# The softmax sums' steps of a fused FNet and window-attention kernel placed farther apart, and the first projection rows prepared behind the attention instead of inside it

## Chip, cores and metric

One core of a Trainium2 chip. The metric is the device time of one launch in microseconds. All times below are of the kernel before the change, and all line numbers in this part are those of its profile.

## What is computed

The sequence has S = 2048 rows of D = 512, in f32. A gate mixes a Fourier mixing layer with sliding-window attention:

```python
a = x @ dft_hid_re.T;  b = x @ dft_hid_im.T
y = dft_seq_re @ a - dft_seq_im @ b                    # spectral branch
q, k, v = split(x @ wqkv)                              # 32 heads of 16
scores = q @ k.T / 4,  kept where 0 <= i - j < 256
o = softmax(scores) @ v @ wo                           # attention branch
g = sigmoid((x * gate_w).sum(-1))
out = g * y + (1 - g) * o
```

The DFT matrices are inputs, loaded as cr and ci. All products run as three matmuls on split operands: each f32 operand is cast to a high part (a CAST on ACT) and a low part (a subtraction on DVE), and high by high, high by low and low by high are added up in PSUM.

## The kernel before

**The loop.** Attention goes over 128 blocks k (8 groups of 4 heads by 16 row blocks of 128 keys), each in two half blocks p = 0, 1. The loop counts n; the row maxima of block n are worked out 11 blocks ahead of block k = n - 11. A half block holds: scores for the row maxima (PE L426, DVE L430, "s_pair"), a piece of the dense stream ("fill"), the transposed scores (PE L486), their exp (ACT L489) and the window's mask (POOL L492 and L496), and pieces of the dense stream again. Every few blocks a "visit" multiplies by v (PE L513). The dense stream holds the projections, the spectral branch and, towards the end, the long DFT products `dc` (PE L270 and L282), whose operands are loaded as `raw` from cr and ci and split at L653. What is done per four blocks is called a u (0 to 31).

**The row maxima's way.** The maxima of four blocks (`rows`) go through DRAM: `m_scr<-rows`, then two loads `ring0<-m_scr`, which put them into the operand of the t matmuls at L486.

**The row sums' way.** After the last visit of u = k//4 - 1, eight steps stand in the list `later`, each at a number of half blocks counted from 2n: o_take (ACT copies the block o out of PSUM, L528, into a buffer `os` or `ev`), o_store (SP stores four rows of sums to `l_scr`, 8 KB), o_sums (SP loads them as 128x16), o_turn (DVE reciprocal, L541), o_back (SP stores them), o_load (SP loads them broadcast into an `ev`), o_out (POOL multiplies, L555) and o_end (four SP stores to `o_scr`). The buffers: `os` is one of the two v tiles' space vst0 and vst1 for u from 2 to 23, else one of the five `ev` buffers, which the spectral branch's pieces (`r_scr`) use as well.

**What sets the order.** While attention runs, every engine works in the order in which the code is written (a manual schedule). SP issues nearly all transfers (helper at L60) in that one order, so a transfer that has to wait for its buffer or its data holds all behind it. At the end of attention, `attention_done` closes the manual schedule for all engines but PE; what is written behind that point is placed by a scheduler on the other engines.

**The end.** The output projection (L1008 its products, seven instead of eight per pair of row blocks, by sums and differences) works on pairs of row blocks. A pair needs its rows of o (`oraw<-o_scr`), their sums (POOL L959 to L962; of the first pair DVE does them), their split (ACT and DVE, L84 and L89) and `rt`, loaded from r_scr, into which DVE adds the result (L1012). `tail_step` counts steps t of the dense stream behind attention, and BEGIN lists the step at which each pair's products begin. LAST is the number of the pair (15, 14), whose row block 15 is finished by the kernel's last 12 matmuls (L631). Tokens (L289, L308, L312, L613) are tiny ACT copies that mark when a `dc` bank is free again; PE waits for them.

**The first pair's preparation.** In the kernel before, the load of the first pair's rows (first_load), their sums (first_sums, on DVE) and splits (split_a(0), first_split) are called inside the attention loop, at blocks 124 to 128, by the dictionary BEFORE_END.

Of the kernel before, what the change touches and what calls it, by code (L numbers as in the profile page):

```python
# [7 lines left out]
F32 = mybir.dt.float32  # L8
# [6 lines left out]
P = 128  # L15
# [3 lines left out]
NG = 4  # L19
# [5 lines left out]
HV = 17  # L25
# [3 lines left out]
WARM = 10  # L29
BEHIND = 5  # L30
SWITCH = 7
LAST = 5
FILL_FIRST, FILL_PAIR, FILL_T = 12, 16.3, 12


# [1 line left out]
def fnet_window_mix(ctx: ExitStack, tc: tile.TileContext, xT, x, wqk, wv, wr, wi, cr, ci, wo, gw, out):  # L37
    nc = tc.nc

    const = ctx.enter_context(tc.tile_pool(name="const", bufs=1))  # L40
# [18 lines left out]
    def ld(dst, src):  # L59
        mark("sp", nc.sync.dma_start(dst, src))  # L60
# [8 lines left out]
    def mark(e, ins):  # L69
        last[e] = ins.ins  # L70

    @contextmanager
    def behind(*engines):
        with ExitStack() as es:
            for e in engines:
                if free and e in last:
                    es.enter_context(tc.issue_after(last[e]))
            yield
# [3 lines left out]
    def split(hi, lo, raw, act=False):  # L82
        if act:
            nc.scalar.copy(hi, raw)  # L84
        else:
            cast = (nc.gpsimd if act is None else nc.vector).tensor_copy(hi, raw)
            if act is None:
                mark("pool", cast)
        return nc.vector.tensor_sub(lo, raw, f(hi))  # L89
# [104 lines left out]
    vst = [const.tile([P, 8 * NG, HV], F32, name=f"vst{b}") for b in range(2)]  # L194
# [108 lines left out]
    def all_rows():  # L303
        H = Halves
        if H.part not in H.ended:
            while H.upper and H.upper[0][0] < H.part:
                pop()
            nc.scalar.copy(token, H.ps[:1, :1])  # L308
        while H.upper:
            pop()  # L310
        if H.part not in H.ended:
            nc.scalar.copy(token, H.ps[:1, :1])  # L312
        while H.due:
            H.due.pop(0)[1]()
        H.whole = True
# [205 lines left out]
    sums_t = [const.tile([P, 16], F32, name=f"sums{i}") for i in range(2)]  # L521

    def o_take(u):
        if 2 <= u < 24:
            o = const.tile([P, 8 * NG * HV], F32, name="os", tag=f"vst{u % 2}")[:, :512]
        else:
            o = ev.tile([P, 512], F32, name="ev")
        mark("act", nc.scalar.copy(o, OT.pop()))  # L528
        OS[u] = [o]
# [317 lines left out]
    def tail_step():  # L847
        t = next(clock)
        for i, begin in enumerate(BEGIN):
            if t == begin + 2:  # L850
# [7 lines left out]
            if i > 3 and t == max(0, begin - 9):  # L858
                wo_load(i)

    BEGIN = range(2, 26, 3)

    def flat(i):
        return ring[i].rearrange("r p s -> r (p s)")
# [6 lines left out]
    def os_spot(m, b, n=1):  # L871
        if m == 6 and b:
            at_c = 3 * S + 528
        else:
            at_c = (4 + m % 3 + 3 * (m == 6)) // 2 * S + 16 + 512 * ((m % 3 + (m == 6)) % 2) + 1024 * b
        t = flat(0 if m < 3 or m == 6 and b else 1)[:, at_c:at_c + 512 * n]
        return t if n == 1 else t.rearrange("p (m s) -> p m s", m=n)

    def halves(t):
        if len(t.shape) == 2:  # L880
            return t[:, :256], t[:, 256:]
        if len(t.shape) == 3:
            return t[:, :, :256], t[:, :, 256:]
        return t[:, :, :, :256], t[:, :, :, 256:]
# [7 lines left out]
    def wo_fetch(c):  # L892
        RAW[c] = [const.tile([P, 8 * NG * HV], F32, name="tw", tag=f"vst{j}")[:, :512] for j in range(2)]
        for j in range(2):
            ld(RAW[c][j], wo[j][:, HALVES[c]])
# [3 lines left out]
    def spare():  # L899
        return quarters(spared, 4)  # L900
# [8 lines left out]
    def fin_split(c, m):  # L909
        split(fin(m, 0, c), fin(m, 1, c), DIFF[c][m], True)  # L910

    def attention_done():
        all_rows()
        in_order.close()
        free.append(True)
        last.clear()
        ctx.enter_context(tc.manual_schedule(engines={mybir.EngineType.PE}))
        while later:
            later.pop(0)[1]()
        RT.append(const.tile([P, 6, 512], F32, name="rt", tag="home"))  # L920
        new = const.tile([P, NB * 4 * HV + 16], F32, name="oraw", tag="vall"), \
            at.tile([P, 4, WIN], F32, name="pt", bufs=4).rearrange("p a b -> p (a b)")
        ORAW[:0] = [t[:, 512 * c:512 * c + 512] for t in new for c in range(2)]
        r_load(0)
        wo_load(1)
        r_load(1)
        for i in range(2, 4):
            wo_load(i)
        FIN.append(True)
# [7 lines left out]
    def wo_load(i):  # L937
        pair = [15, 14] if i == LAST else [wait.pop(0) for _ in range(2)]
        raw = []
        for tb in pair:  # L940
            raw.append(ORAW.pop(0))
            ORAW.append(raw[-1])
            ld(raw[-1].rearrange("p (g t) -> p g t", g=NG),
               o_scr[tb // 4][:, :, tb % 4 * P:tb % 4 * P + P].rearrange("g p t -> p g t"))
        O[i] = pair, raw

    def first_load():
        ORAW.extend(const.tile([P, 8 * NG * HV], F32, name="oraw", tag=f"vst{b}")[:, :512] for b in range(2))
        wo_load(0)

    def r_load(i):
        k = 4 if i == LAST else i % 2 * 2
        R[i] = RT[0][:, k], RT[0][:, k + 1]
        for tb, t in zip(O[i][0], R[i]):
            with behind("sp"):
                ld(t, r_scr[2 if i == LAST else 1][tb])

    def sums(eng, s1, s2, s3, s4, a, b):
        eng.tensor_add(s1, b[:, :256], b[:, 256:])  # L959
        eng.tensor_sub(s3, a[:, :256], b[:, :256])  # L960
        eng.tensor_sub(s2, s1, a[:, :256])
        eng.tensor_sub(s4, a[:, 256:], s2)  # L962
# [9 lines left out]
    def first_sums():  # L972
        EX[0] = spare()
        sums(nc.vector, *EX[0], *O[0][1])

    def split_a(i):
        a, b = O[i][1]
        split(*halves(os_spot(0, i % 2, 2)), a.rearrange("p (m t) -> p m t", m=2), True)
        split(*halves(os_spot(2, i % 2)), b[:, 256:], True)

    def first_split(m):
        split(*halves(os_spot(m, 0)), EX[0][m - 3], True)
# [14 lines left out]
    def wo_begin(i):  # L997
# [27 lines left out]
        def rest():  # L1025
# [8 lines left out]
            for tb, r in zip(pair, (r1, r2)):  # L1034
                if i == LAST:
                    mixed[tb] = r
# [46 lines left out]
    summed = 0  # L1083
    later = []

    BEFORE_END = {(124, 1): first_load, (126, 1): first_sums, (127, 0): lambda: split_a(0)}
    for c, k in enumerate((111, 117)):
        BEFORE_END[k, c] = lambda c=c: wo_fetch(c)
        BEFORE_END[k + 2, 1 - c] = lambda c=c: wo_diffs(c)
        for j, m in enumerate((0, 1, 2, 4, 6, 5, 3)):  # L1090
            at_j = 2 * (k + 3) - c + j
            BEFORE_END[at_j // 2, at_j % 2, 0] = lambda c=c, m=m: fin_split(c, m)
    for j, m in enumerate((3, 5, 4, 6)):
        BEFORE_END[((127, 0, 0), (127, 1), (127, 1, 0), (128, 0))[j]] = lambda m=m: first_split(m)

    def ahead_of_end(*key):
        if key in BEFORE_END:
            with behind("t", "sp"):
                BEFORE_END[key]()

    for n in range(NU + LAG + 1):
        k = n - LAG
        ring_ahead(n + 1)
        if n % 4 == 1 and 9 <= n < 25:
            c = n // 4 - 2
            need(("v", 4 * c + 3))
            v_load(c)
        due = k > summed and (k % 4 == 0 or k == NU or k % 2 == 0 and not more)
        for p in range(2):
            if n < NU:  # L1110
                s_pair(n, p)
            fill(n)
            if p and due:
                visit(summed, k)
                summed = k
                if k % 4 == 0:
                    u = k // 4 - 1
                    G, sb = divmod(u, 4)
                    if G < 2 * NG - 1:
                        for c in [sb - 1] * (sb > 0) + [3] * (sb == 3):  # L1120
                            v_load(4 * (G + 1) + c)
                    later += [(2 * n + at, lambda do=do, u=u: do(u)) for at, do in
                              ((2, o_take), (3, o_store), (5, o_sums), (7, o_turn), (8, o_back), (10, o_load),
                               (13, o_out), (15, o_end))]
                    later.sort(key=lambda x: x[0])
                if k < NU:
                    t_pair(k, 0)
            if 0 <= k < NU and (p or not due):
                t_pair(k, p)
            ahead_of_end(k, p)  # L1130
            ahead_of_end(k, p, 0)
            fill(n)
            for at_n, at_p, do in TURN:
                u, j = divmod(n - at_n, 4)
                if p == at_p and j == 0 and 0 <= u < 32:
                    do(u)
            while later and later[0][0] <= 2 * n + p:
                later.pop(0)[1]()
# [47 lines left out]
```

## Time and profile before

| | us |
|---|---|
| median of 3 runs | 898.5 (895.81 to 898.92) |
| the profiled execution | 901.72 |
| its span | 900.0 |
| PE busy | 856.3 |
| DVE, ACT, POOL busy | 544.3, 405.1, 278.3 |
| moved by DMA | 167.62 MB, mean 186 GB/s |

The mean granted clock of PE was 0.979. The span begins with the first instruction and ends with the last transfer. The waits are lists of "engine line waited for: us in total, times, longest us"; SPq is SyncE's queue, whose instructions issue transfers. In the timelines a row is start, length, engine, line, operation, tiles (out<-in), and in brackets the idle time before it with what ended it. From about 74 us to 788 us the program is in the attention loop; from there on it is in the tail.

### The profile page before, as it was taken

Reading aid. Unit: us, or ns where it says so; the run is one execution under the profiler, and the core shown is the slowest. Engines: PE = TensorE matmul, PEld = TensorE weight load, DVE = VectorE, ACT = ScalarE, POOL = GpSimd, SP = SyncE. Lnnn points to the kernel's source line nnn. Section 1 sums busy time; section 2 is a strip of 40 time slices with the busy share of each in tenths; the row PEclk is TensorE's granted clock in tenths of the full one; section 3 lists DMA queues with packets and bytes.
Section 4 is the critical chain, followed back from the end, with each engine's and each line's share of the span. In section 5 each row is a group of like instructions: output and inputs, shape, how many; then the busy total and the mean of one; then the engine's idle time right before and its main releaser. Section 6 shows DMA issues by size and latency. Waiting matters only on the chain.

```text
span 900.0 us, 21479 instructions
## 1 busy us (share of the span) xinstructions
PE 856.3 (95%) x7641; PEld 734.0 (82%) x7641; DVE 544.3 (60%) x1607; ACT 405.1 (45%) x1017; POOL 278.3 (31%) x561
## 2 busy tenths in 40 slices
PE   8999999999989999999999999989899999949998
PEld 7988887777866888889999889868698887738987
DVE  5485666665656566656656666635567675536873
ACT  4423554445533454555455544433254456522320
POOL 7001223233322233333233332322234335423420
PEclk9999999999999999999999999989999999979999
DMA  7988688768778328765666569888786744566721
GB/s 231 254 233 203 168 202 246 236 169 221 208 184 251 87 80 217 176 146 140 165 163 166 160 193 278 211 206 285 194 199 173 208 131 121 154 174 214 235 94 71
DMA packets 110123, 167.62 MB, mean 186 GB/s; under 512 B 38720, under 2 KB 48448, under 8 KB 110016
## 3 DMA queue, kind: packets, MB, share of 16 engines
q1 hardware_dynamic: 109584, 165.60, 67.0%
q8 instruction: 60, 0.98, 0.5%
q10 hardware_dynamic: 432, 0.66, 0.3%
q14 instruction: 47, 0.39, 0.1%
HBM read 113.51 MB, written 52.69 MB: 185 GB/s over the span
## 4 chain that ended last, share of the span: by engine, by line
PE 72%; DMA 15%; DVE 5%; ACT 3%; issue 2%; SPq 2%; POOL 0%; DVEq 0%; ACTq 0%; POOLq 0%
PE dc L270 28%; PE dab L270 8%; PE o L513 7%; PE dqk L270 7%; PE s L426 5%; PE dv L270 4%; PE t L1008 4%; PE t L486 4%; PE dc L282 4%; DMA l_scr<-os 3%; DMA qk_scr<-home 2%; DMA ring<-qk_scr 2%; SPq L60 2%; DVE junk L430 2%; DMA raw<-ci 1%
## 5 line engine op out<-in xcount | busy, mean ns | idle before, releaser
L430 DVE CUSTOM_DVE_ANT_0 junk<-s,mask 128x384 bf16<-128x384 f32 (+2 forms) x512 | 270.4, 528 | 164.0 <-PE s L426 104.5
L270 PE MATMUL dc<-big,hi 64*128 64x512 f32 x1802 | 362.7, 396 | 3.4 <-ACT hi L653 3.4
L270 PEld LDWEIGHTS dc<-big,hi 64*128 64x128 f32 x1802 | 240.8, 188 | 10.9 <-ACT hi L653 3.8
L270 PE MATMUL dc<-big,lo 64*128 64x512 f32 x900 | 248.0, 396 | 0.3 <-DVE lo L653 0.2
L489 ACT ACTIVATE pt<-t 128x384 f32<-128x384 f32 (+2 forms) x400 | 164.1, 475 | 132.6 <-PE t L486 118.4
L492 POOL TENSOR_SCALAR_AFFINE_SELECT pt<-pt 128x256 f32<-128x256 f32 x200 | 86.8, 434 | 396.7 <-ACT pt L489 370.3
L270 PEld LDWEIGHTS dc<-big,lo 64*128 64x128 f32 x900 | 134.8, 188 | 3.8 <-DVE lo L653 1.1
L426 PE MATMUL s<-ring,ring 48*128 48x384 f32 (+2 forms) x512 | 127.8, 349 | 4.3 <-ACT pt L489 2.0
L653 DVE TENSOR_TENSOR lo<-raw,hi 128x512 fp32r<-128x512 f32 x142 | 106.7, 755 | 23.9 <-ACT hi L653 17.4
L653 ACT CAST hi<-raw 128x512 fp32r<-128x512 f32 x142 | 87.9, 626 | 73.1 <-PE dc L270 28.4
L270 PE MATMUL dab<-hi,big 64*128 64x512 f32 x512 | 116.5, 409 | 3.9 <-DVE home L98 3.4
L270 PE MATMUL dqk<-big,hi 64*128 64x512 f32 x480 | 112.8, 395 | 1.5 <-DVE home L96 1.0
L486 PE MATMUL t<-ring,ring 50*128 50x384 f32 (+2 forms) x512 | 108.9, 347 | 5.4 <-DVE ml L430 5.3
L426 PEld LDWEIGHTS s<-ring,ring 48*128 48x128 f32 x512 | 85.1, 187 | 18.5 <-DVE ml L430 6.1
L270 PE MATMUL dab<-lo,big 64*128 64x512 f32 x256 | 94.9, 405 | 0.0
L486 PEld LDWEIGHTS t<-ring,ring 50*128 50x128 f32 x512 | 68.3, 186 | 24.9 <-DVE ml L430 11.3
L270 PE MATMUL dqk<-big,lo 64*128 64x512 f32 x240 | 88.6, 398 | 0.0
L270 PEld LDWEIGHTS dab<-hi,big 64*128 64x128 f32 x512 | 78.4, 192 | 9.4 <-DVE home L98 4.9
L270 PEld LDWEIGHTS dqk<-big,hi 64*128 64x128 f32 x480 | 73.0, 185 | 8.2 <-DVE home L98 2.3
L496 POOL TENSOR_SCALAR_AFFINE_SELECT pt<-pt 128x256 f32<-128x256 f32 x176 | 74.5, 423 | 0.0
L513 PE MATMUL o<-pt,vall 128*32 128x384 f32 (+2 forms) x1104 | 72.6, 393 | 0.9 <-POOL pt L492 0.9
L489 ACT ACTIVATE home<-t 128x384 f32<-128x384 f32 (+2 forms) x112 | 45.4, 469 | 51.8 <-PE t L486 48.7
(120 smaller groups left out, 1069.0 us busy)
## 6 DMA issues: line engine op xcount, KB each, us to landing
qk_scr<-home SPq DMA_DIRECT2D x64, 256.0 KB
ring<-qk_scr SPq DMA_DIRECT2D x128, 128.0 KB
raw<-cr SPq DMA_DIRECT2D x32, 512.0 KB
raw<-ci SPq DMA_DIRECT2D x32, 512.0 KB
r_scr<-ev SPq DMA_DIRECT2D x44, 256.0 KB
ab_scr<-home SPq DMA_DIRECT2D x20, 512.0 KB
big<-ab_scr SPq DMA_DIRECT2D x20, 512.0 KB
ring<-qk_scr SPq DMA_DIRECT2D x128, 64.0 KB
```

The source lines that it names most:

```text
L60: mark("sp", nc.sync.dma_start(dst, src))
L270: nc.tensor.matmul(ps, lhsT[r], rhs[r], start=start, stop=stop, tile_position=(64 * i, 0), skip_group_check=True)
L282: return nc.tensor.matmul(ps, lhsT, rhs, start=start, stop=stop, skip_group_check=True)
L426: nc.tensor.matmul(pss[h][:, :w], ring[0][r, pair, j * BQ:(j + 1) * BQ], ring[1][r, pair, k0:k0 + w], start=True, stop=True, tile_position ...
L430: mark("dve", nc.vector.tensor_tensor_reduce(out=junk[:, :w], in0=pss[h][:, :w], in1=mask[:, WIN - w:], scale=1.0, scalar=3e38, op0=OP.add ...
L486: nc.tensor.matmul(pss[h][:, :w], ring[1][r, pair, q0:q0 + BQ], ring[0][r, pair, q0:q0 + w], start=True, stop=True, tile_position=(64 * h, 0))
L489: mark("t", nc.scalar.activation(pt[:, 2 * p + h, :w], pss[h][:, :w], AF.Exp, scale=-1.0))
L492: nc.gpsimd.affine_select(a, a, pattern=[[0, 2], [1, 128]], compare_op=OP.is_ge, fill=0.0, base=0, channel_multiplier=-1)
L496: nc.gpsimd.affine_select(a, a, pattern=[[0, 2], [-1, 128]], compare_op=OP.is_gt, fill=0.0, base=0, channel_multiplier=1)
L513: nc.tensor.matmul(OT[0][32 * t:32 * t + 32, q - sb * 512:e - sb * 512], vall[:, 4 * HV * kb + HV * t:4 * HV * kb + HV * t + 32], PT[n][:, ...
L653: return fn(*args)
L1008: nc.tensor.matmul(ps, o[:, a, c], fin(n, b, c), start=start and c == 0 and a + b == 0, stop=c == 1 and a == 1, skip_group_check=True)
```

## The change

1. The steps' places in half blocks behind 2n go from 2, 3, 5, 7, 8, 10, 13, 15 to 2, 3, 6, 9, 10, 13, 17, 19 (o_take, o_store, o_sums, o_turn, o_back, o_load, o_out, o_end).
2. The copies rotate over three buffers: vst0, vst1 and an `ev`, by u % 3, up to u = 24 (from 25 on all are `ev`).
3. first_load, first_sums, split_a(0) and the first_splits are no longer called inside the loop but in attention_done, behind the close of the manual schedule, and the list `later` is emptied behind the loads of rt and of the next pair's rows, not ahead of them.
4. BEGIN goes from steps 2, 5, 8, ... 23 to 6, 9, 12, ... 27, and LAST from 5 to 4.

```diff
-LAST = 5
+LAST = 4
...
     def o_take(u):
-        if 2 <= u < 24:
-            o = const.tile([P, 8 * NG * HV], F32, name="os", tag=f"vst{u % 2}")[:, :512]
+        if 2 <= u < 25 and u % 3 < 2:
+            o = const.tile([P, 8 * NG * HV], F32, name="os", tag=f"vst{u % 3}")[:, :512]
...
-    BEGIN = range(2, 26, 3)
+    BEGIN = range(6, 30, 3)
...
         ctx.enter_context(tc.manual_schedule(engines={mybir.EngineType.PE}))
-        while later:
-            later.pop(0)[1]()
         RT.append(const.tile([P, 6, 512], F32, name="rt", tag="home"))
...
+        first_load()
         ORAW[:0] = [t[:, 512 * c:512 * c + 512] for t in new for c in range(2)]
         r_load(0)
         wo_load(1)
         r_load(1)
+        while later:
+            later.pop(0)[1]()
+        first_sums()
+        split_a(0)
+        for m in (3, 5, 4, 6):
+            first_split(m)
...
-    BEFORE_END = {(124, 1): first_load, (126, 1): first_sums, (127, 0): lambda: split_a(0)}
+    BEFORE_END = {}
...
-    for j, m in enumerate((3, 5, 4, 6)):
-        BEFORE_END[((127, 0, 0), (127, 1), (127, 1, 0), (128, 0))[j]] = lambda m=m: first_split(m)
...
                     later += [(2 * n + at, lambda do=do, u=u: do(u)) for at, do in
-                              ((2, o_take), (3, o_store), (5, o_sums), (7, o_turn), (8, o_back), (10, o_load),
-                               (13, o_out), (15, o_end))]
+                              ((2, o_take), (3, o_store), (6, o_sums), (9, o_turn), (10, o_back), (13, o_load),
+                               (17, o_out), (19, o_end))]
```

Three places show what this does to the order. The first is SP's order around block 120 of attention, before: `l_scr27` and `l_scr28` are the scratch rows of u = 27 and 28, `sums` their tiles, `m_scr31` the last row maxima.

```order
L60 DMA ev_11119<-l_scr27_196 128x1x512
L60 DMA tw_11138<-wo 128x512
L60 DMA tw_11139<-wo 128x512
L60 DMA l_scr28_197<-ev_11121 4x512
L60 DMA m_scr31_168<-rows_11153 32x128
L60 DMA raw_11195<-ci 128x1024
L60 DMA sums0_322<-l_scr28_197 128x16
L60 DMA ev_11230<-r_scr2_9_246 128x512
L60 DMA r_scr1_7_228<-ev_10984 128x512
L60 DMA o_scr3_204<-ev_10792 16x512 x4
L60 DMA ring0_287<-m_scr31_168 2x2x512 x2
```

The same place on SP after the change:

```order
L60 DMA l_scr28_197<-ev_11115 4x512
L60 DMA m_scr31_168<-rows_11147 32x128
L60 DMA raw_11193<-ci 128x1024
L60 DMA ev_11202<-l_scr27_196 128x1x512
L60 DMA ev_11228<-r_scr2_9_246 128x512
L60 DMA r_scr1_7_228<-ev_10983 128x512
L60 DMA sums0_322<-l_scr28_197 128x16
L60 DMA ring0_287<-m_scr31_168 2x2x512 x2
L60 DMA raw_11328<-ci 128x1024
```

The broadcast load of u 27 now stands directly ahead of the load `ev_11228<-r_scr2_9`, which uses the same one of the five buffers, so that load can only go out when u 27 has been multiplied; the sums of u 28 and the ring loads stand behind it.

The second place is POOL's order at the same blocks, where the product of u 27 is the row L555; the selects on `home_321` are of blocks 118 and 119, those on `pt` of block 120 and later. Before:

```order
L492 AFFINE_SELECT home_321<-home_321 128x2x128
L496 AFFINE_SELECT home_321<-home_321 128x2x128
L555 TENSOR_TENSOR ev_10792<-ev_10792,ev_11119 128x512
L492 AFFINE_SELECT home_321<-home_321 128x2x128
L496 AFFINE_SELECT home_321<-home_321 128x2x128
```

And after:

```order
L492 AFFINE_SELECT pt_11307<-pt_11307 128x2x128
L496 AFFINE_SELECT pt_11307<-pt_11307 128x2x128
L492 AFFINE_SELECT pt_11307<-pt_11307 128x2x128
L496 AFFINE_SELECT pt_11307<-pt_11307 128x2x128
L555 TENSOR_TENSOR ev_10786<-ev_10786,ev_11202 128x512
L492 AFFINE_SELECT pt_11346<-pt_11346 128x2x128
```

The product has moved behind the selects of block 119 and the four of block 120.

The third place is ACT's order in attention's last two blocks (126: the exps with 128x256; 127: those with 128x128). Before, with `oraw_11566` and `oraw_11567` the rows of the first pair:

```order
L489 ACTIVATE pt_11636<-t_11638 128x256
L289 COPY token_305<-dc_11515 1x1
L489 ACTIVATE pt_11636<-t_11657 128x256
L489 ACTIVATE pt_11636<-t_11658 128x256
L653 CAST hi_11676<-raw_11572 128x512
L613 COPY token_305<-dc_11421 1x1
L489 ACTIVATE pt_11688<-t_11689 128x128
L489 ACTIVATE pt_11688<-t_11690 128x128
L84 CAST ring0_287<-oraw_11566 128x2x256
L84 CAST ring0_287<-oraw_11567 128x256
```

After, with `oraw_11820` and `oraw_11821`:

```order
L489 ACTIVATE pt_11630<-t_11632 128x256
L289 COPY token_305<-dc_11509 1x1
L84 CAST ring0_287<-oraw_11820 128x2x256
L84 CAST ring0_287<-oraw_11821 128x256
L489 ACTIVATE pt_11630<-t_11651 128x256
L489 ACTIVATE pt_11630<-t_11652 128x256
L84 CAST ring1_288<-spare_324 128x256 x2
L653 CAST hi_11666<-raw_11561 128x512
```

The first pair's casts, although they are written behind attention, were placed ahead of the second half of block 126's exps. On SP their load now stands here:

```order
L60 DMA o_scr0_201<-ev_11115 16x512 x4
L60 DMA l_scr30_199<-ev_11595 4x512
L60 DMA raw_11660<-ci 128x1024
L60 DMA ev_11669<-l_scr29_198 128x1x512
L60 DMA ev_11691<-r_scr2_10_247 128x512
L60 DMA sums0_322<-l_scr30_199 128x16
L60 DMA oraw_11820<-o_scr0_201 128x4x128
L60 DMA oraw_11821<-o_scr0_201 128x4x128
```

It stands behind the stores of u 28's product and behind the load of the sums of u 30.

## Prediction

> **What bounds the kernel now.** I read the page first, for the engine that is full; then the waits of PE, for what its idle time is owed to; then the waits of SP, because SP issues nearly every transfer in one order; then the chain and the timelines at the places that the change moves.
>
> ```profile
> PE 856.3 (95%) x7641; PEld 734.0 (82%) x7641; DVE 544.3 (60%) x1607; ACT 405.1 (45%) x1017; POOL 278.3 (31%) x561
> PE dc L282 <- ACT token L312: 12.2, 1, 12.2
> PE t L486 <- DVE ml L430: 5.3, 11, 1.3
> PE dab L270 <- DVE home L98: 3.4, 2, 2.7
> PE dc L270 <- ACT hi L653: 3.4, 1, 3.4
> PE t L1008 <- DVE rt L1012: 2.0, 1, 2.0
> PE s L426 <- ACT pt L489: 2.0, 2, 1.7
> SPq L60 <- DMA l_scr<-os: 69.8, 21, 7.3
> ```
>
> The columns of the waits are the total, the number and the longest, in us. PE is busy 856.3 of 900.0 us, and the change gives it no matmul more or less. So everything that can be won or lost is PE's idle time: 43.7 us, of which one wait of 12.2 us at attention's end is the largest, and 14.1 us (5.3 + 3.4 + 3.4 + 2.0) stand in the middle behind row maxima, evictions and operands. SP waits 69.8 us for the stores of the row sums' first step to land (21 of them), before it can issue the load of their second. These waits cost PE time only where something that PE needs stands behind them. The chain of work between 583 and 647 us shows that place:
>
> ```profile
> 583.46 7.87 DMA l_scr<-os
> ...
> 607.63 10.02 DMA l_scr<-os
> ...
> 637.88 7.75 DMA raw<-ci
> 646.40 0.74 PE dc L270 x4
> ```
>
> Start and length in us. Two stores of 8 KB take 7.87 and 10.02 us to land; SP stands there, and what is behind it comes late: in the end raw for the cast at L653, for which PE waits 3.4 us at 646.40.
>
> **The change part by part.** The sum is made against the profiled execution (901.72 us, span 900.0), which is 3.2 us above the median of the runs, 898.5; the same difference is then taken off the median.
>
> *1. The steps farther apart, in the middle of attention.*
>
> ```profile
> L486 PE MATMUL t<-ring,ring x512: 218/336/685, 74.5 to 781.6; 50*128 50x384 f32 x149, 50*128 50x256 f32 x11, 50*128 50x128 f32 x11
> ```
>
> Two of these matmuls belong to a half block, so 256 half blocks start in 707.1 us: 2.8 us each. Store to load goes from 2 to 3 half blocks, 5.6 to 8.4 us: of a landing of 7.87 us nothing is left to wait for, of one of 10.02 us some 1.6. Reading back to multiplying goes from 3 to 4. Nothing is added: the same copies, stores, loads, reciprocals and products. The three buffers hold a copy 17 to 19 half blocks (48 to 53 us) instead of 13 to 15; copies of one u use one of three buffers, which comes round after three u, 24 half blocks (67 us), so a buffer is free in time, and where it is of the five ev buffers the order gives the slot to others only after the product.
>
> What PE gets of it lies between zero (the lateness has other causes: the bare DMA time stays, and raw itself took 7.75 us) and the 14.1 us above. The stores are not the only thing in the way: 11 of the waits are for row maxima, 0.5 us on average, which the DVE's own load explains. I count the single wait of 3.4 us at 646.40 in full, and a third of the other 10.7 us as owed to SP; that would be 7.0, of which I keep 5, since part of each is late for the next cause at once. **−5 us**, bounds −9 and +1 (above nothing, because other transfers are now packed at other places).
>
> The Trainium skill (page "DMA: Bandwidth & Descriptors", section "Anatomy of one DMA — SWDGE (gpsimd) path") gives a transfer about 2.0 us fixed and its bytes by 436 GB/s. By that an estimate for 8 KB is 2.0 us, which two half blocks already covered, and this term would be nothing. The landings of 7.87 and 10.02 us speak against it in this stage; a store at 799.01, shown below, takes 1.68 us and agrees, in a stage with hardly any traffic.
>
> *2. A new stall at block 122.* Product 27 (POOL, L555) moves behind the selects of block 120, and SP's load `ev_11228<-r_scr2_9` takes the buffer that this product reads. What is queued behind this load on SP is the sums of u 28 and then both transfers `ring0<-m_scr31`, which bring the row maxima that the t matmuls of block 122 need. Before:
>
> ```profile
> 749.53 1.50 POOL L555 TENSOR_TENSOR ev<-ev 128x512 f32<-128x512 f32 x1
> 759.20 0.59 POOL L496 TENSOR_SCALAR_AFFINE_SELECT pt<-pt 128x256 f32<-128x256 f32 x1
> 751.05 0.33 SPq L60 DMA_DIRECT2D ev<-r_scr  x1
> 761.62 0.34 PE L486 MATMUL t<-ring,ring 50*128 50x384 f32 x2
> ```
>
> The product ended at 751.03 and SP went on at 751.05. Now it can start at 759.79, behind the select of 759.20, and ends at 761.1 (L555 takes 1.26 to 1.50 us here). The load, one store, the sums' load and the two ring loads are issued by about 762.8 (0.33 us each for such a load, to 0.6), and a ring load needs about 2 us to land (the bound below is 1.7, of a light queue, above it 4.2, the chain's `DMA ring<-m_scr` in the loaded stage):
>
> ```profile
> 596.81 4.23 DMA ring<-m_scr
> 799.01 1.68 DMA l_scr<-ev
> ```
>
> So PE starts block 122 at about 764.8 instead of 761.62: **+3.2 us**, bounds +2 and +6. DVE's reciprocal of u 28 waits beside it, behind the same SP, and raw for the next cast too; both fit into the same shift.
>
> *3. Attention's end.* Two things are moved against each other here, and the gap of 12.2 us absorbs some of it.
>
> ```profile
> 774.67 0.41 POOL L496 TENSOR_SCALAR_AFFINE_SELECT home<-home 128x256 f32<-128x256 f32 x1
> 777.36 0.66 ACT L489 ACTIVATE pt<-t 128x256 f32<-128x256 f32 x2
> 778.88 0.66 ACT L489 ACTIVATE pt<-t 128x256 f32<-128x256 f32 x2 [0.84 <-PE t L486]
> 780.67 0.93 ACT L84 CAST ring<-oraw 128x512 fp32r<-128x512 f32 x2
> 781.59 0.22 PE L486 MATMUL t<-ring,ring 50*128 50x128 f32 x2
> 784.31 0.67 DVE ring L89 x2
> 795.60 0.39 PE L270 MATMUL dc<-big,hi 64*128 64x512 f32 x1
> 796.89 1.26 POOL L555 TENSOR_TENSOR ev<-ev 128x512 f32<-128x512 f32 x1 [13.46 <-DMA ev<-l_scr]
> 801.15 0.93 SPq L60 DMA_DIRECT2D oraw<-o_scr  x2
> 803.98 0.62 ACT L84 CAST ring<-oraw 128x512 fp32r<-128x512 f32 x1 [13.85 <-DMA oraw<-o_scr]
> 808.01 0.14 ACT L312 COPY token<-dc 1x1 f32<-1x1 f32 x1
> ```
>
> Before, the casts of the first pair's rows stood behind the exps of block 127's first half, and their data was there. Now they stand ahead of the exps of 126's second half. Their load stands on SP behind the stores of product 28, which now follows the select of 774.67 and ends at 776.4 (775.08, and 1.3 for a product), then behind its four stores to o_scr, about 1.8 us, and the sums of u 30, whose store is issued at 778.2 and lands 1.7 us later, at about 780 (1.68 above). So the load goes out at about 781 and lands at 784 (oraw took 2.83 us from 801.15 to 803.98). ACT stands from 778.05 to 784, and with it the exps that free the t tiles: the t matmuls of 127's second half come at 785.6 instead of 781.59, **+4.0**, and the low halves cast after it, on DVE (two pairs of pieces, 0.67 us a pair by the row of 784.31, ahead of the dense stream's own), make it about +5.4 for the last visit (bounds +3 and +8). With that the dense matmuls behind the last visit, which ended at 796.0, end at 801.4.
>
> The gap itself ends with the token at L312 on ACT, which stands behind the second pair's casts and the sums of POOL. Before: product 30 waits for its broadcast, 13.46 us, the stores of o follow it on SP, and only then, at 801.15, comes the load. Now the load stands ahead of the last sums' steps but behind the stores of product 29 and behind six loads of rt, pt and oraw; I put it at about 799, landed by 802.5, and the token at 808.5, against 808.01 before. So the gap falls from 12.2 to 7 us, and the 5.4 us are spent ahead of it: **+0.4 net**, bounds −3 and +4.
>
> *4. The wait for rt at the first product goes.*
>
> ```profile
> 816.87 4.99 DMA rt<-r_scr
> 822.49 1.70 PE t L1008 x12
> ```
>
> The first product's output is added into rt, whose load came behind the last sums at 816.87. Now the loads stand ahead of them (about 798), and the products start later against the dense matmuls. **−2.0 us**; bounds −2.0 and 0, if raw is late next.
>
> *5. The last pair's end.* With LAST one lower, the last pair's products stand directly ahead of the final 12 matmuls; before, 24 dense matmuls (5.48 us) lay between.
>
> ```profile
> 889.67 5.48 PE dc L282 x24
> 895.15 1.44 PE t L631 x12
> 890.29 0.81 SPq L60 DMA_DIRECT2D out<-rt  x2
> HBM read 113.51 MB, written 52.69 MB: 185 GB/s over the span
> ```
>
> So the stores issued at 890.29, hidden before, are issued about 5 us later, just ahead of the last ones. Two of 256 KB at the span's mean of 185 KB per us are 2.8 us; they have about 1.4 us, the final matmuls, to themselves, and may run faster than the mean where nothing else is under way: **+0.7**, bounds 0 and +1.5.
>
> Sum: −5 + 3.2 + 0.4 − 2.0 + 0.7 = **−2.7 us**, which makes 899.0 of the profiled 901.72 and **895.8 of the median**.
>
> **The rivals.**
>
> *The new waits win (slower).* One mechanism: SP's one order. Product 27's lateness (10 us on SP) isn't worked off in the six blocks that are left, so that the first pair's rows land later than 784, with ACT's casts in the exps' way; from about 786 on the token at L312 is delayed as much as PE. Price: 5 for block 122, 4 for the end, 1 for the last stores, −2 for rt, with the middle giving nothing: +8, 906.5. For it: the product stands ten microseconds later with nothing in between that waits less. Against it stands the stage's row by stretches, whose DMA share is 0.47, so that SP has room:
>
> ```profile
> 720.00:800.00 80.00, 73.78 (x691) 57.35 (x687) 40.41 (x91) 42.53 (x118) 33.05 (x61) 0.99 0.47 139
> ```
>
> *The middle gives all (faster).* Then −9 there, +2 for block 122, −2 at attention's end, since the second pair's rows come at 797 already, −2 for rt: −11, 887.5. For it: every wait of SP for l_scr in the waits is shorter than 8.4 us. Against it: SP waits for much else.
>
> *The spacing buys nothing.* Stores land in 2 us wherever nothing else is loaded, and PE's waits in the middle stay, since transfers of raw and ring are what is slow there: 0 + 3.2 + 0.4 − 2.0 + 0.7 = +2.3, 900.8. This is where the page's fixed price leads. The two chain rows of 7.87 and 10.02 speak against it, the 7.75 us of raw for it.
>
> **How the numbers follow.** I give my forecast 0.40, the slower case 0.27, the faster one 0.20 and the case of nothing gained 0.13. Faster by over 0.5% is under 894.0 us, slower over 903.0; about 0.5% is what a measurement of this kernel can tell from no change. The forecast's own range is 890 to 902 with a third of it under 894, so faster is 0.20 + 0.14 = 0.34; slower is 0.27 with 0.02 from the others, 0.29; the same is 0.37. Half of the faster case lies under 887 and a third of the slower one over 908, which leaves out 2 in 10: 887 to 908.
>
> **What would show it.** Right in term 1: SP's waits for `l_scr<-os` fall from 69.8 us to under 25, and the 3.4 us wait of dc for hi is gone. Right in term 2: a wait of SP for POOL's L555 of some 10 us near 751 to 761, and PE waiting 2 to 6 us at the t matmuls of block 122. Right in term 3: ACT waits 5 to 6 us for `oraw<-o_scr` between the exps of block 126, and PE's wait for the token at L312 is 5 to 9 us. Right in term 4: no wait of L1008's line for rt at the first product. Right in term 5: the span goes on longer after PE's last matmul. The prediction is wrong if PE's busy time moves by more than 2 us, if a granted clock other than before's is seen, or if PE waits in the middle of attention are as large as before while SP's are gone.

## The result and the profile after

The changed kernel takes 901.97 us (median of 18 runs, 899.55 to 907.82) against 894.5 us of 18 runs of the kernel before (888.59 to 900.04): ratio 1.0086, 95% interval 1.0066 to 1.0107. It is slower by 0.9%, 7.5 us; 895.8 with a range of 887 to 908 was forecast, on the other side of no change.

The profiled execution took 904.15 us, span 902.4, only 2.4 us more than the span before, because the profile of before is of an execution slower than most of its kernel (901.72 against a median of 894.5). A second profile of before (e0_before) took 901.37. The comparison of traces below shows where time went; how much of it holds for most executions, the timed experiments say.

Busy times of the page, after:

```profile
PE 854.2 (95%) x7641; PEld 731.5 (81%) x7641; DVE 554.9 (61%) x1607; ACT 404.6 (45%) x1017; POOL 285.4 (32%) x561
```

PE's waits, after (us in total, times, longest), the five that matter here:

```profile
PE dc L282 <- ACT token L312: 9.6, 1, 9.6
PE t L486 <- ACT pt L489: 7.8, 1, 7.8
PE s L426 <- DVE ml L430: 3.9, 11, 1.0
PE t L486 <- DMA ring<-m_scr: 3.1, 1, 3.1
PE dc L270 <- ACT hi L653: 0.7, 1, 0.7
```

SP's three longest, in the same columns:

```profile
SPq L60 <- DVE lo L653: 57.5, 27, 10.8
SPq L60 <- ACT ev L762: 28.7, 13, 4.1
SPq L60 <- DMA ev<-l_scr: 25.9, 11, 5.1
```

SP's 69.8 us for stores to l_scr are off the list of its 17 longest waits (the last of which has 9.6); 3.8 us are left of them. It now waits most for the low halves at L653, that is, for a raw buffer to come free: SP is ahead of its work, where it was behind. The 3.4 us wait of dc for hi has become 0.7. Two new waits of PE are among the longest, 7.8 and 3.1 us.

Start of the transposed scores (L486) of some blocks, and PE's end, from the rows of PE's matmuls in each kernel's profile. The steps are named narrow (old) or wide (new), for u below 24 and from 24:

| kernel | steps, early/late | end | block 120 at | 120 to 124 | 124 to 127's second half | from there to PE's end | ratio to before, 95% |
|---|---|---|---|---|---|---|---|
| before | narrow/narrow | old | 756.6 | 15.4 | 9.5 | 115.0 | 1 |
| e0_before | the same | old | 759.2 | 15.4 | 9.5 | 112.1 | (one run) |
| after | wide/wide | new | 747.7 | 20.5 | 17.5 | 113.0 | 1.0086 (1.0066 to 1.0107) |
| e1_mid | wide/narrow | old | 750.2 | 15.5 | 9.5 | 111.5 | 0.9942 (0.9915 to 0.9968) |
| e11_store | one wider/narrow | old | 747.9 | 15.4 | 9.5 | 112.9 | 0.9964 (0.9937 to 0.9991) |
| e2_end | narrow/narrow | new | 753.7 | 15.5 | 20.2 | 111.7 | 1.0091 (1.0060 to 1.0122) |
| e3_late_short | wide/narrow | new | 745.6 | 15.5 | 19.1 | 112.8 | 1.0066 (1.0041 to 1.0091) |
| e4_casts_last | wide/wide | new, ACT held | 750.9 | 22.1 | 9.5 | 118.6 | 1.0077 (1.0049 to 1.0105) |
| e5_hold | wide/wide | new, held | 746.6 | 21.2 | 9.5 | 112.6 | 1.0022 (0.9997 to 1.0047) |
| e6_token | wide/narrow | old, token first | 747.0 | 15.4 | 9.5 | 112.5 | 0.9984 (0.9961 to 1.0008) |
| e7_begin | narrow/narrow | BEGIN, LAST alone | 749.4 | 15.5 | 9.5 | 112.2 | 1.0002 (0.9976 to 1.0027) |
| e8_both | wide/narrow | new, held, token first | 750.9 | 15.4 | 9.5 | 107.0 | 0.9903 (0.9870 to 0.9937) |
| e9_turn | wide/narrow | as e8, reciprocal later | 748.3 | 15.4 | 9.5 | 103.1 | 0.9913 (0.9879 to 0.9947) |
| e10_late_wide | wide/wide | as e8 | 748.0 | 21.9 | 9.5 | 111.6 | 0.9995 (0.9962 to 1.0028) |

The changed kernel is 8.9 us ahead at block 120, loses 5.0 us by block 124 and 8.0 more by the second half of 127, and the tail gives back only 2.0. The stretches from 120 to 127 agree within 0.1 us among the kernels with narrow late steps and the old end, so they can be read from one profile; block 120 itself scatters by 10 us among kernels with the same steps, and needs the timed runs.

The first loss, on POOL, SP and PE, after:

```profile
750.85 1.29 POOL L555 TENSOR_TENSOR ev<-ev 128x512 f32<-128x512 f32 x1
752.17 0.34 SPq L60 DMA_DIRECT2D ev<-r_scr  x1
753.50 0.66 SPq L60 DMA_DIRECT2D ring<-m_scr  x2
756.01 0.83 PE L486 MATMUL t<-ring,ring 50*128 50x384 f32 x2 [3.15 <-DMA ring<-m_scr]
```

The product of u 27 ends, SP goes on 0.03 us later, the ring loads land about 2.5 us after their issue, and block 122 starts. This is the chain of term 2, link by link. What the prediction left out stands in the granted clock (columns: busy us, matmuls, clock, DMA share, GB/s):

```profile
747.73:752.80 5.07, 5.07 (x48) 1.00 0.00 0
756.01:759.00 2.99, 2.99 (x15) 0.51 0.66 233
759.00:762.00 3.00, 3.00 (x27) 0.92 0.22 49
785.70:790.98 5.28, 5.28 (x26) 0.57 0.00 0
811.60:814.60 3.00, 3.00 (x7) 0.50 0.16 38
```

For some 3 us behind the gap PE runs at half its clock, and again behind the next two gaps. The 3.15 us of waiting cost 5.0 us.

The second loss and the gap at attention's end, after:

```profile
773.48 0.66 ACT L489 ACTIVATE pt<-t 128x256 f32<-128x256 f32 x2
775.35 0.44 SPq L60 DMA_DIRECT2D raw<-ci  x1
775.88 0.55 SPq L60 DMA_DIRECT2D ev<-l_scr  x1
776.48 0.48 SPq L60 DMA_DIRECT2D ev<-r_scr  x1
777.54 0.92 SPq L60 DMA_DIRECT2D oraw<-o_scr  x2
784.17 0.62 ACT L84 CAST ring<-oraw 128x512 fp32r<-128x512 f32 x1 [10.01 <-DMA oraw<-o_scr]
785.70 0.74 PE L486 MATMUL t<-ring,ring 50*128 50x128 f32 x2 [7.83 <-ACT pt L489]
799.84 0.98 SPq L60 DMA_DIRECT2D oraw<-o_scr  x2
805.69 0.62 ACT L84 CAST ring<-oraw 128x512 fp32r<-128x512 f32 x1 [9.59 <-DMA oraw<-o_scr]
811.60 0.80 PE L282 MATMUL dc<-big,hi 128*128 128x512 f32 x1 [9.62 <-ACT token L312]
```

ACT stands 10.01 us at the first pair's cast, with the exps behind it that PE needs. The load took 6.6 us from issue to the cast's start, not 2.8: raw (512 KB) and two loads of 256 KB went out just ahead of it. The gap at the token is 2.6 us shorter than before, but it starts later by more.

### The profile page after: what moved, and what is told of

It reads as the page before. It is cut to its first block, busy times and chain, and to the rows that moved or that the text cites. A ratio compares the mean times of both kernels' runs of the same rounds, so it can differ in the third digit from the quotient of the medians.

```text
span 902.4 us, 21525 instructions
## 1 busy us (share of the span) xinstructions
PE 854.2 (95%) x7641; PEld 731.5 (81%) x7641; DVE 554.9 (61%) x1607; ACT 404.6 (45%) x1017; POOL 285.4 (32%) x561
## 4 chain that ended last, share of the span: by engine, by line
PE 71%; DMA 14%; DVE 6%; SPq 3%; issue 3%; ACT 2%; POOL 1%; DVEq 0%; ACTq 0%; POOLq 0%
PE dc L270 26%; PE dqk L270 8%; PE o L513 8%; PE dab L270 6%; PE dc L282 5%; PE s L426 4%; PE t L486 4%; PE t L1013 4%; PE dv L270 4%; SPq L60 3%; DVE junk L430 3%; DMA ring<-qk_scr 2%; DMA raw<-ci 2%; DMA raw<-cr 2%; DMA oraw<-o_scr 1%
## 5 line engine op out<-in xcount | busy, mean ns | idle before, releaser
L270 PE MATMUL dc<-big,lo 64*128 64x512 f32 x900 | 250.8, 397 | 0.0
L492 POOL TENSOR_SCALAR_AFFINE_SELECT pt<-pt 128x256 f32<-128x256 f32 x200 | 88.0, 440 | 432.7 <-ACT pt L489 402.1
L653 ACT CAST hi<-raw 128x512 fp32r<-128x512 f32 x142 | 87.6, 624 | 80.2 <-DMA raw<-ci 29.5
L653 DVE TENSOR_TENSOR lo<-raw,hi 128x512 fp32r<-128x512 f32 x142 | 105.5, 746 | 26.7 <-ACT hi L653 26.0
L486 PE MATMUL t<-ring,ring 50*128 50x384 f32 (+2 forms) x512 | 105.8, 347 | 13.5 <-ACT pt L489 7.8
L270 PE MATMUL dab<-hi,big 64*128 64x512 f32 x512 | 112.0, 397 | 2.6 <-DVE home L96 1.7
L426 PEld LDWEIGHTS s<-ring,ring 48*128 48x128 f32 x512 | 83.1, 184 | 26.0 <-DVE ml L430 10.6
L486 PEld LDWEIGHTS t<-ring,ring 50*128 50x128 f32 x512 | 67.4, 186 | 31.7 <-issue 15.3
L270 PE MATMUL dab<-lo,big 64*128 64x512 f32 x256 | 91.6, 392 | 0.0
L270 PEld LDWEIGHTS dab<-hi,big 64*128 64x128 f32 x512 | 75.5, 185 | 8.4 <-DVE home L96 3.0
L496 POOL TENSOR_SCALAR_AFFINE_SELECT pt<-pt 128x256 f32<-128x256 f32 x176 | 75.7, 430 | 0.0
```

Source lines behind the costliest of these rows:

```text
L270: nc.tensor.matmul(ps, lhsT[r], rhs[r], start=start, stop=stop, tile_position=(64 * i, 0), skip_group_check=True)
L426: nc.tensor.matmul(pss[h][:, :w], ring[0][r, pair, j * BQ:(j + 1) * BQ], ring[1][r, pair, k0:k0 + w], start=True, stop=True, tile_position ...
L486: nc.tensor.matmul(pss[h][:, :w], ring[1][r, pair, q0:q0 + BQ], ring[0][r, pair, q0:q0 + w], start=True, stop=True, tile_position=(64 * h, 0))
L492: nc.gpsimd.affine_select(a, a, pattern=[[0, 2], [1, 128]], compare_op=OP.is_ge, fill=0.0, base=0, channel_multiplier=-1)
L496: nc.gpsimd.affine_select(a, a, pattern=[[0, 2], [-1, 128]], compare_op=OP.is_gt, fill=0.0, base=0, channel_multiplier=1)
L653: return fn(*args)
```

## The experiments

The theories after the first comparison. A: the wide steps gain in the middle, and the losses come only because the wide late steps make the first rows late. B: the new end costs by itself, whatever the steps. C: the lead at block 120 is chance between executions. None of the kernels leaves out a part of the computation.

**e1_mid**: steps wide for u below 24 alone, with the change's three buffers (o_take as in the change); everything behind as before.

```diff
-((2, o_take), (3, o_store), (5, o_sums), (7, o_turn), ...
+zip((2, 3, 6, 9, 10, 13, 17, 19) if u < 24 else (2, 3, 5, 7, 8, 10, 13, 15),
+    (o_take, o_store, o_sums, o_turn, o_back, o_load, o_out, o_end))]
```

> The kernel before with the wide steps and the three buffers for u below 24 only; the last eight u and the whole end as before. Theory A (the wide steps gain in the middle, the loss is all behind block 120): 3 to 5 us faster than before, ratio 0.994 to 0.997; PE's waits at attention's end as before, a wait of about 12 us for the token at L312, none of more than 1 us at block 122. Theory C (the middle's lead in the profile of the change is chance between executions): ratio 0.998 to 1.002.

Measured: 891.63 us, ratio 0.9942 (0.9915 to 0.9968). Theory C falls: the middle's gain is real, 5.2 us. It is the gain of steps and buffers together; no run has one without the other.

**e2_end**: the change with the old steps and buffers.

```diff
-        if 2 <= u < 25 and u % 3 < 2:
+        if 2 <= u < 24:
...
-((2, o_take), (3, o_store), (6, o_sums), (9, o_turn), ...
+((2, o_take), (3, o_store), (5, o_sums), (7, o_turn), ...
```

> The change without its steps: steps and buffers as before, but the first pair's preparation behind the close of the order, BEGIN 6 and LAST 4. Theory A (the end costs only because the wide steps make the first rows late): no wait of PE for exps at block 127, no wait for the row maxima at block 122, the wait for rt at the first product gone; ratio 0.996 to 1.002. Theory B (the new end costs by itself): ratio 1.006 to 1.010, with the loss behind 785 us.

Measured: 1.0091 (1.0060 to 1.0122). **Theory A falls**: with the old steps, and so with early rows, the new end costs as much as the whole change. ACT in its profile:

```profile
773.57 0.62 ACT L84 CAST ring<-oraw 128x512 fp32r<-128x512 f32 x1 [8.91 <-DMA oraw<-o_scr]
775.65 0.40 ACT L84 CAST ring<-oraw 128x256 fp32r<-128x256 f32 x1 [1.41 <-DMA oraw<-o_scr]
778.19 0.40 ACT L84 CAST ring<-spare 128x256 fp32r<-128x256 f32 x1 [0.60 <-DVE spare L967]
778.50 1.63 ACT L489 ACTIVATE home<-t 128x384 f32<-128x384 f32 x4
```

With rows that are earlier, the scheduler put the casts earlier too, now ahead of block 124's exps, and they wait all the same, 8.91 us. PE loses 3.3 and 3.6 us there, and blocks 124 to 127 take 20.2 us instead of 9.5.

**e3_late_short**: the change with narrow steps from u 24.

```diff
-((2, o_take), (3, o_store), (6, o_sums), (9, o_turn), ...
+zip((2, 3, 6, 9, 10, 13, 17, 19) if u < 24 else (2, 3, 5, 7, 8, 10, 13, 15),
```

> The change with the wide steps for u below 24 only; the last eight u have the old steps, the end is the new one. Theory A: both stalls (3.1 us at block 122, 7.8 us at block 127) are gone and the middle's gain stays: ratio 0.991 to 0.997, 9 to 13 us under the change. Theory B: 1.003 to 1.007, the end's cost less the middle's gain. Theory C: 0.997 to 1.002.

Measured: 1.0066 (1.0041 to 1.0091), as B said; the stall at block 122 is gone (15.5 us), that before the exps is not (19.1).

**e4_casts_last**: in the change, the first pair's sums and casts are issued behind the last exps of attention.

```diff
+        exp = last["t"]
...
+        with tc.issue_after(exp):
             first_sums()
             split_a(0)
```

> The change with one thing held: the first pair's sums and casts are issued behind the last exps of attention. Theory A: PE's wait of 7.8 us for exps at block 127 goes, with the slower matmuls behind it; the wait for the token at L312 grows from 9.6 to 11 to 14 us; the 3.1 us at block 122 stay: 5 to 9 us under the change, ratio to before 0.998 to 1.003. If the load's lateness is what counts and the order of the casts is not, the wait only moves to the token at L312, and the ratio stays at 1.006 to 1.010.

Measured: 1.0077 (1.0049 to 1.0105), no gain. The wait for exps is gone (9.5 us from 124 to 127), but its place is taken, though not at L312:

```profile
PE dc L282 <- ACT token L312: 8.1, 1, 8.1
PE dc L270 <- DVE lo L653: 7.4, 1, 7.4
```

DVE, in the same profile, stood at the pair's sums, which the order had ahead of the low halves that PE needs:

```profile
790.25 0.43 DVE L966 TENSOR_TENSOR spare<-oraw 128x256 f32<-128x256 f32 x1 [11.93 <-DMA oraw<-o_scr]
791.72 1.28 DVE L653 TENSOR_TENSOR lo<-raw,hi 128x512 fp32r<-128x512 f32 x2
```

**e5_hold**: held on DVE as well, behind those low halves.

```diff
-        with tc.issue_after(exp):
+        with tc.issue_after(exp), tc.issue_after(lo):
```

> The change with the first pair's sums and casts held on both engines: on ACT behind the last exps, on DVE behind the low halves that the last blocks' dense matmuls need. Theory B' (the new end costs because the preparation, placed by the scheduler, stands ahead of attention's own work and its data comes late): no wait of PE between block 123 and the last visit, about 10 us from block 124 to 127 as before; the 3.2 us at block 122 stay; 5 to 9 us under the change, ratio to before 0.998 to 1.003. If it is the load's lateness alone, the time moves to the token at L312 and the ratio stays at 1.006 to 1.010.

Measured: 1.0022 (0.9997 to 1.0047). Against the change that is 0.994 (0.990 to 0.997 if the two intervals are taken as independent): some 6 us come back by the place of these few instructions alone, with the same steps, and with SP's 985 transfers in the same order in the traces of the change, of e4_casts_last and of e5_hold. PE's waits:

```profile
PE t L486 <- DMA ring<-m_scr: 3.5, 1, 3.5
PE dc L270 <- ACT token L289: 3.1, 1, 3.1
PE dc L282 <- ACT token L312: 2.9, 1, 2.9
```

As expected there is none between block 123 and the last visit; the 3.1 us for the token at L289 come directly behind that visit.

**e6_token**: e1_mid, with the second pair's preparation behind the token at L312.

```diff
-            nc.scalar.copy(token, H.ps[:1, :1])
+            mark("tok", nc.scalar.copy(token, H.ps[:1, :1]))
...
+                with tc.issue_after(TOK[0]):
                     wo_split(i)
```

> The middle's wide steps with the old end (as in e1_mid), and the second pair's sums and casts issued behind the token at L312. If the gap of 11.6 us is owed only to the token's place on ACT: the gap falls to under 5 us and the ratio to 0.985 to 0.989. If the first products wait for rt next, which lands at about 815 us behind the last sums, the time comes back there: a wait of 6 to 9 us at L1008's line, and the ratio stays at 0.991 to 0.995.

Measured: 0.9984 (0.9961 to 1.0008), not better than e1_mid and outside both expected ranges. The gap is gone, and its time stands at the first products:

```profile
PE t L1011 <- DVE rt L1015: 7.2, 1, 7.2
PE t L1011 <- ACT pt L1020: 4.2, 1, 4.2
```

**e7_begin**: before, with BEGIN and LAST of the change.

```diff
-LAST = 5
+LAST = 4
...
-    BEGIN = range(2, 26, 3)
+    BEGIN = range(6, 30, 3)
```

> The kernel before with BEGIN and LAST of the change alone; the preparation stays in the loop, the steps stay narrow. By the terms of the prediction: the wait of 2.0 us for rt goes, the last stores cost 0.4 us: ratio 0.996 to 1.000. If later products cost by themselves (theory B): 1.003 or more.

Measured: 1.0002 (0.9976 to 1.0027): nothing either way.

**e8_both**: the new end with narrow late steps, held as in e5_hold, and the token first as in e6_token: the three edits above, put together.

```diff
+zip((2, 3, 6, 9, 10, 13, 17, 19) if u < 24 else (2, 3, 5, 7, 8, 10, 13, 15),
...
+        with tc.issue_after(exp), tc.issue_after(lo):
             first_sums()
...
+                with tc.issue_after(TOK[0]):
                     wo_split(i)
```

> The change with wide steps for u below 24 only, the first pair's preparation held as in e5_hold, and the second pair's behind the token at L312 as in e6_token; rt is loaded ahead of the last sums. Theory B': no stall from block 120 to the last visit, the gap at L312 under 5 us: ratio 0.982 to 0.989, the best of all. If raw for the pieces behind it comes too late, a wait of dc for hi or lo of 5 to 8 us takes the gap's place: 0.990 to 0.995.

Measured: 0.9903 (0.9870 to 0.9937), 885.68 us: the best ratio, ahead of both kernels. Its profile has a wait of 5.5 us for lo in place of the gap, so the second expectation is nearer:

```profile
PE dc L282 <- DVE lo L653: 5.5, 1, 5.5
```

**e9_turn**: as e8_both, with the last reciprocal, which DVE stood at, issued later.

```diff
-        while later:
+        while len(later) > 5:
             later.pop(0)[1]()
...
         t = next(clock)
+        if t == 5:
+            with tc.issue_after(last["lo"]):
+                while later:
+                    later.pop(0)[1]()
+            for i in range(2, 4):
+                wo_load(i)
```

> As e8_both, with the last reciprocal (u 31), which stood ahead of the low halves that PE waited 5.5 us for, issued behind a later one, and raw loads ahead of its steps. If that reciprocal's place on DVE is what is late next: the wait of dc for lo falls under 2 us, ratio 0.983 to 0.987. If DVE's or SP's work behind it is the limit, the wait comes back at the first products or at raw: 0.989 to 0.992.

Measured: 0.9913 (0.9879 to 0.9947). The 5.5 us are gone from the profile (span 880.2), but the median, 885.46 us, is that of e8_both. The profiled execution, 881.87 us, is near the lower end of the 12 runs (880.34 to 891.15); whether a gain of up to some 3 us is there stays open.

**e10_late_wide**: e8_both with wide steps for all u.

```diff
-zip((2, 3, 6, 9, 10, 13, 17, 19) if u < 24 else (2, 3, 5, 7, 8, 10, 13, 15),
+zip((2, 3, 6, 9, 10, 13, 17, 19),
```

> As e8_both, with the wide steps for all u, the last eight too. By the stall at block 122 (3.1 to 3.5 us and slower matmuls behind it: block 120 to 124 took 20.5 and 21.2 us in the change and in e5_hold, 15.4 to 15.5 with narrow late steps): 4 to 6 us above e8_both, ratio 0.994 to 0.998. If the gap behind attention absorbs it, as the prediction had it for part of the loss: 0.989 to 0.992.

Measured: 0.9995 (0.9962 to 1.0028), 0.9% above e8_both: the wide late steps alone cost about 8 us (4 to 12 if the two intervals are taken as independent), more than expected. In the profiles, block 120 to 124 takes 21.9 us against 15.4, and the stretch behind attention is longer too, 111.6 against 107.0: it absorbs nothing.

**e11_store**: e1_mid, where only store to load is wider.

```diff
-zip((2, 3, 6, 9, 10, 13, 17, 19) if u < 24
+zip((2, 3, 6, 8, 9, 11, 14, 16) if u < 24
```

> As e1_mid, but for u below 24 only the distance from store to load is wider (3 half blocks); the others are the old ones, one half block later. If SP's wait for the 8 KB stores is what the wide steps take away (term 1 of the prediction): ratio 0.993 to 0.997, like e1_mid. If the other waits count as much: 0.997 to 1.001.

Measured: 0.9964 (0.9937 to 0.9991); the interval overlaps that of e1_mid. SP's waits in its profile:

```profile
SPq L60 <- DMA l_scr<-ev: 34.7, 13, 6.7
SPq L60 <- DMA l_scr<-os: 31.1, 11, 7.2
```

The ratio is in the first expected range, but not for its reason: the waits for the stores fell from 83.3 us (69.8 and 13.5) only to 65.8. So the gain doesn't hang on these waits alone; which part of the steps or the buffers brings it is not shown.

**e0_before**: the kernel before once more, one run.

> The kernel before once more, for a second profile. If the profiled execution of 901.72 us had more idle time in the middle than most: block 120 is reached 3 to 8 us earlier than at 756.6 us, and the single waits of 2.7 us at 258 and 3.4 us at 646 are not there or shorter. If the middle is the same in all executions: within 1 us of it.

Measured: 901.37 us, and the same gaps as in the first profile:

```profile
PE dc L282 <- ACT token L312: 12.3, 1, 12.3
PE dc L270 <- ACT hi L653: 3.8, 1, 3.8
PE dab L270 <- DVE home L98: 3.6, 2, 2.8
```

My expectation of a faster middle was wrong: the waits recur in both profiles, and block 120 comes 2.6 us later still. But the wait of 2.0 us for rt at the first product, my term 4, isn't there.

## Why the prediction was wrong, by its steps

**Term 1, the middle: right in size and sign, not in its way, so the size is luck in part.** −5 was said; e1_mid gives −5.2 (−7.6 to −2.9). The prediction let the sums' load go out 8.4 instead of 5.6 us behind their store, so that a landing of 7.87 us would be covered. SP's time doesn't go by half blocks of the list: for u from 2 to 23 the load went out 6.5 us behind the store before and 4.4 us after (medians), sooner and not later, and still SP's waits for the stores were gone. e11_store has the same three half blocks and kept the waits (6.7 us from store to load). What differs is the order on SP: in e11_store each of these 22 stores is issued directly behind the broadcast load of the u before, 256 KB, in e1_mid each stands ahead of it. The same u, first in e11_store, then in e1_mid:

```profile
355.78 0.55 SPq L60 DMA_DIRECT2D ev<-l_scr  x1
356.43 0.50 SPq L60 DMA_DIRECT2D l_scr<-ev  x1
363.22 0.32 SPq L60 DMA_DIRECT2D sums<-l_scr  x1
355.83 0.52 SPq L60 DMA_DIRECT2D l_scr<-ev  x1
357.73 0.55 SPq L60 DMA_DIRECT2D ev<-l_scr  x1
360.47 0.38 SPq L60 DMA_DIRECT2D sums<-l_scr  x1
```

That the large load ahead of the store makes it late fits these rows and the first pair's load in term 3; no run moves the store alone. The fit that term 1 cites from the Trainium skill is for transfers issued by GpSimd, while SP issued these. (A slip without weight: the copies are held 15 to 17 half blocks, not 17 to 19, since o_take stands at 2.)

Part of what came off PE was not idle time but half clock behind it. The clock of the kernel before, behind its wait of 2.70 us that ends at 257.94 (busy us, matmuls, clock, DMA share, GB/s):

```profile
257.94:259.94 2.00, 2.00 (x14) 0.79 0.23 54
259.94:261.90 1.96, 1.96 (x12) 0.50 0.97 237
```

From block 28 to 40 the profile of before took 76.3 us, that of after 71.3, with a mean granted clock of 1.00 from 233 to 304 us. Other profiles agree: the four kernels with narrow early steps took 74.1 to 77.8 us there, the ten with wider ones 69.7 to 72.9. From block 40 to 120, where I had placed the 3.4 us in full, the two took 443.2 and 443.5: nothing. The other 4 us of the lead at block 120 lie ahead of block 28, where e7_begin, with narrow steps, is as early as the change.

**Term 2, block 122: the mechanism right, the size not.** The stall was 3.15 us (+3.2 said); with the clock behind it 5.0. e10_late_wide prices the wide late steps at about 8 us in all where nothing else stalls.

**Term 3, attention's end: this is the step that failed**, +0.4 said and +7.3 measured from 127's first half to the restart behind the token (35.4 us in the profile after, 28.1 before). The last visit came 9.8 us late, not 5.4, and the gap shrank by 2.6 us, not by 5.2. The mechanism up to the load was right: on before's clock (127's first half starts 3.9 us earlier after), ACT was ready for the cast at 778.0 and the load went out at 781.4, both as said; its data came at 788, not 784. Three things were wrong. The first pair's load was given the 2.83 us of a free queue, while about 1 MB had been issued within 2.2 us ahead of it: 6.6 us. The slower matmuls behind the gap were left out, 1.8 us up to the last visit. And the gap was taken for a buffer that absorbs what comes ahead of it. It wasn't: the second pair's load stands in the same SP order, behind raw, which waits for the low halves of the very block that was held up:

```profile
790.05 0.35 SPq L60 DMA_DIRECT2D raw<-ci  x1
```

Behind the first pair's load of 777.54 SP issued nothing for 11.6 us, so the gap's end moved with its start. e4_casts_last, e5_hold and e2_end show the cause together: the preparation stands ahead of attention's own work, on ACT and on DVE, and waits for its data wherever the scheduler puts it; held behind it, on both engines, it costs 6 us less.

**Terms 4 and 5.** The wait for rt was one execution's: e0_before, e1_mid and e11_store, with the old end, don't have it. e7_begin, which has the later products and the last pair's place but not the earlier loads of rt, finds nothing; −1.3 was said for both terms. The last stores cost 0.4 us more from PE's end to the span's end (3.8 against 3.4), within the bounds.

**The rival that came true** is the slower one: new waits at block 122 and in the exps' way, 906.5 said, with the middle giving nothing. Its mechanism for the end was SP's order and the casts, which is what the trace shows, but its condition (the first rows later than 784) wasn't needed: the change met it, at 788 on before's clock, while e2_end has the rows earlier and loses as much. It was wrong that the middle gives nothing, and its 906.5 is 4.5 us too high. I gave it 0.27; the order of ACT, which stood in my own text, spoke for more.

**The basis.** 3.2 us were taken off for the profiled execution; with more runs it was 7.2. That doesn't change the sign. One sign that the prediction named for itself appeared at its edge: PE's busy time moved by 2.1 us, 2 was the limit.

## What to carry to other kernels

When work is moved out of a written order to a scheduler, look first at what it now stands ahead of on every in-order engine, and price its wait by what is issued ahead of its load, not by the load alone. A later idle gap absorbs a delay only if what ends the gap doesn't hang on the delayed work; here it did, by one queue. And a gain and a loss that come in one change are worth separating: the early steps with their buffers alone are 0.6% faster, and the whole change with its late steps narrow, its first preparation held and the second pair's behind the token 1.0%. A distance in a list of steps is no distance in time on a queue: look at what stands directly ahead of a transfer.

## What the runs showed of the hardware

After each of PE's gaps of 2.70, 3.15, 7.83, 9.62 and 12.22 us the granted clock was 0.5 for some 3 to 6 us; after gaps of 1.69 and 2.00 us it stayed at 1.00. After the gap of 12.22 us, and after 2.00 us, in the kernel before:

```profile
808.21:811.20 2.99, 2.99 (x7) 0.50 0.73 217
822.49:824.50 2.01, 2.01 (x15) 1.00 0.06 25
```

But the length of a gap alone doesn't decide. In the profile after, the clock fell as well behind a gap of 1.58 us that ended at 560.73:

```profile
561.51:564.92 3.41, 3.41 (x29) 0.50 0.91 262
```

At block 122 a wait of PE of 3.15 us (the change), 3.26 (e4_casts_last), 3.50 (e5_hold) and 3.59 (e10_late_wide) made the stretch from 120 to 124 longer by 5.0 to 6.7 us. The Trainium skill (page "TensorE: Matmul & The Clock Gate", section "HAM oscillation — how this bites in real kernels") has as a rule that PE should not idle for over about 3.4 us at a time. The direction agrees; here 2.70 us, and once 1.58 us, were enough.
